# Zero rows only for tokens that no expert keeps, stored under the branch behind the slots, and two small clearings that close the slots' work

## The chip, the cores and the metric

The kernel runs on one core of a Trainium2 chip. The metric is the time of one execution on the device, in microseconds; lower is better. The core has five engines with instruction streams of their own: TensorE (PE in the profile, its weight loads PEld), VectorE (DVE), ScalarE (ACT), GpSimd (POOL) and SyncE (SP). POOL and SP also issue most of the DMAs. The engines wait for each other, and for DMAs, through semaphores. A letter q behind an engine's name (POOLq) is its sequencer, which runs branches, register loads, waits and the issue of DMAs.

## The reference

Attention with a threshold, then a mixture of experts in which each token goes to one expert and an expert keeps at most `capacity` tokens. A token that is not kept gets a row of zeros.

```python
# q, k, v: 4 batches x 8 heads x 576 x 64; tau 0.02; 2304 tokens, DM 512, 8 experts, F 1024, capacity 576
scores = q @ k.T / sqrt(64)
scores = where(scores >= max(scores) - tau, scores, -1e9)
x = (exp(scores - max) / sum) @ v                      # rows of 512 per token
expert = argmax(x @ w_gate); gate_w = softmax(x @ w_gate)[expert]
for i in range(2304):                                  # in order of the tokens
    if counts[expert[i]] < capacity: keep[i] = True; counts[expert[i]] += 1
out = zeros((2304, 512))
out[i] = gate_w[i] * (relu(x[i] @ w1[e]) @ w2[e])      # for kept tokens only, e = expert[i]
```

## The kernel before

**Stages.** Attention runs first, for 16 pairs of heads. The gate then gives each token its expert and its rank in it (`emit_gate1` to `emit_gate2`), and GpSimd scatters the rows of x into a buffer `xd` in device memory, sorted by expert (`emit_scatter`, tiles `xr` and `xrt`). The experts' work is done in 21 slots of 128 rows. Slots 0 to 7 are early ones, one for each expert, whose rows are known before the last batch is done. Slots 8 to 20 are late ones (tiles `latey`, `latex`, `hw`, `lateh`); tables that VectorE works out when the counts of all experts are known (`emit_most` to `emit_own`) say which rows and which expert's weights they take. Ten more slots exist as code behind branches (`slow`), for counts that 21 slots don't cover.

**A slot.** GpSimd gathers its rows from `xd` (`emit_gather`), TensorE turns them (`emit_x0`), ScalarE and VectorE split the result into two float16 parts (`emit_x1`, `emit_x2`). F is cut into four chunks. For each chunk c TensorE multiplies by w1 (`emit_a`), ScalarE and VectorE take the ReLU and split it (`emit_h1`, `emit_h2`), for late slots SyncE turns it by a DMA (`emit_hT`), TensorE multiplies by w2 (`emit_b`), and ScalarE (first chunk) or VectorE (the others) adds the scaled result up in the row buffer (`emit_y`). After the last chunk GpSimd stores the slot's rows to their tokens with an indirect DMA (`emit_out`). `scales` (L420) reads gathered rows of late slots in two goes, of eight slots and of five.

**Weights.** Each of the 8 experts' w1 and w2 chunks is a load of 512 KB (`load_w`, issued at L294, tile `ws`, four buffers) that ScalarE and VectorE split into two float16 parts (`split_w`, L305 and L307, tiles `w1b`, `w2b`). The first 14 loads go over SyncE, the other 50 over GpSimd. In the first chunk a split is cut into two halves. "w2 of expert 6" below is that of the first chunk.

**Order.** No order is written out. `Plan.run` simulates the engines with durations, dependencies and priorities given by `T(...)`, and emits the tasks in the order that comes out. A task that is added, removed or given another duration can therefore change the order of all later tasks on every engine. On an engine the order is fixed then: an instruction that waits holds all behind it.

**Zeros.** A row of the output that no slot stores must be zero. In the kernel before, six DMAs (`clear`, L610, 768 KB each) write zeros to the whole output in the middle of the slots' work, and the first `emit_out` comes after them.

**The end.** After the planned work the code goes on with `slow(13)`: a branch (L1417) on the number of half slots, `nhalves`, that is read from the table `nhi` (`emit_nhi`, `emit_nhalves`) to a register of each engine. If it isn't taken, an engine jumps over the slow code to a block that brings its semaphores up to the counts that the slow code would have left, and then to the barrier that closes the program (L1469).

Of the kernel before, what the change touches and what calls it, by code (L numbers as in the profile page):

```python
# [10 lines left out]
F32 = mybir.dt.float32  # L11
# [4 lines left out]
ALU = mybir.AluOpType  # L16
AX = mybir.AxisListType
# [3 lines left out]
P = 128  # L21
QK_SCALE = 64.0
X_SCALE = 16.0
W_SCALE = 64.0
OOB = float(1 << 22)
MC = 4096.0
ROUND = float(2 ** -20)


def view(ap, dims, offset=0):  # L30
    return bass.AP(tensor=ap.tensor, offset=ap.offset + offset, ap=[ap.ap[0]] + [list(d) for d in dims])
# [138 lines left out]
def attention_moe_kernel(ctx: ExitStack, tc: tile.TileContext, q, k, v, tau, w_gate, w1, w2, cap, out):  # L170
    nc = tc.nc
    B, H, S, D = q.shape
    NTOK, DM = out.shape
    E, _, F = w1.shape
# [32 lines left out]
    def const_of(name, shape, dt=F32):  # L207
        return const.tile([P] + shape, dt, name=name)
# [17 lines left out]
    fst = const_of("fst", [5, E])  # L226
    gie = const_of("gie", [E], I32)
    oix = const_of("oix", [NS], I32)
    gsc = const_of("gsc", [NS])

    make_identity(nc, ident)
# [47 lines left out]
    def disjoint(group, ins):  # L279

        i = getattr(ins, "ins", ins)
        tc.declare_no_dep(i, group=group, reason="disjoint rows")
        tc.add_to_no_dep_group(group, i)
# [152 lines left out]
    def open_tables():  # L436
        def tile_of(name, shape, dt=F32):
            tb[name] = pools["tab"].tile([P] + shape, dt, name=name, tag=name)

        for name, shape in (  # L440
            ("most", [E]), ("cut", [NU2 + 1]), ("bl", [2, NU2 + 1]), ("dv", [2, NU2]), ("alone", [1]), ("u", [SLOTS]),
            ("w", [SLOTS]), ("ge", [NL, NU2]), ("pr", [2, NL, NU2]), ("sel", [2, SLOTS]), ("bad", [SLOTS]), ("ex", [SLOTS]),
            ("own", [3, NP]), ("nhs", [1]),
        ):
            tile_of(name, shape)
        for name, shape in (("left", [E]), ("cnt", [NU2]), ("gix", [SLOTS]), ("exi", [SLOTS]), ("nhi", [1])):
            tile_of(name, shape, I32)
        V.memset(tb["cut"][:, 0:1], 0.0)
        V.memset(tb["bl"][:, 0, NU2:], float(1 << 20))
        V.memset(tb["bl"][:, 1, NU2:], 1.0)  # L450
# [122 lines left out]
    def emit_nhi():  # L573
        U = tb["cut"][:, NU2:]
        V.tensor_scalar(out=tb["nhs"], in0=U, scalar1=tb["alone"], scalar2=None, op0=ALU.add)
        V.scalar_tensor_tensor(out=tb["nhi"], in0=U, scalar=2.0, in1=tb["nhs"], op0=ALU.mult, op1=ALU.min)

    def emit_regs(t):
        r = nc.values_load_multi_w_load_instructions(
# [2 lines left out]
        )[1][0]  # L582
        regs.append(r if t < NE + NF else (r, (t - NE - NF) * WE))

    def emit_nhalves():
        gst["nhalves"] = nc.values_load_multi_w_load_instructions(
            tb["nhi"][0:1, 0:1], min_val=0, max_val=2 * SLOTS + E,
            skip_runtime_bounds_check_because="only a comparison reads it",
        )[1][0]

# [14 lines left out]
        )  # L605
        disjoint("out", ins)

    def clear(z, n):

        nc.gpsimd.dma_start(  # L610
            out=out[z * n:(z + 1) * n, :].rearrange("(p t) d -> p t d", p=P),
            in_=view(zero[:, :], [[0, DM // P * n // P], [1, P]]),
        )


    actx = ExitStack()
    if True:
# [357 lines left out]
        def emit_gate1(b, j):  # L975
            G, n = (NJ, P) if j == 0 else (1, P)
            gp = gps.pop((b, j))
            lg = gp[0:n, 2 * P:2 * P + G * E].rearrange("p (g e) -> p g e", e=E)
            rk_ps = gp[0:n, 2 * P + NJ * E:2 * P + (NJ + G) * E].rearrange("p (g e) -> p g e", e=E)
            sm = xp.tile([P, 6, NJ], F32, name="sm", tag="sm")  # L980
            mx, fe, gs, rk, ix, dp = (sm[0:n, i, 0:G] for i in range(6))
            tb = xp.tile([P, 3, NJ, E], F32, name="tb", tag="tb")
            t0, t1, t2 = (tb[0:n, i, 0:G, :] for i in range(3))
            oh = xp.tile([P, NJ + 1, E], F16, name="oh", tag="oh")
            os = oh[0:n, NJ if G > 1 else 0, :]
            oh = oh[0:n, 0:G, :]
            V = nc.vector
            V.tensor_reduce(out=mx, in_=lg, axis=AX.X, op=ALU.max)
            V.tensor_tensor(out=t0, in0=lg, in1=bc(mx, G, n), op=ALU.subtract)
            gst[b, j] = (G, n, rk_ps, mx, fe, gs, rk, ix, dp, t0, t1, t2, oh, os)  # L990
            gst["os", b, j] = TAIL if j else P, os
            gst["bank"] = gp
# [275 lines left out]
        def at(n):  # L1268
            return NU + PM["B0"] + n * PM["SL"]
# [12 lines left out]
        def V1(name, dur, fn, deps, p=0):  # L1282
            T(name, "V", dur, fn, deps, pt + p)
# [26 lines left out]
            V1(("ex", i), 60 + 17 * m, partial(emit_ex, t), [("ge", i)], p + .5)  # L1310
            V1(("exi", i), 280, partial(emit_exi, t), [("ex", i)], p + .5)
        V1(("own",), 600, emit_own, [("gix", 1), ("bad", 1)], 1)
        V1(("nhi",), 280, emit_nhi, [("alone",)], 2)
        for t in range(NE, NS):
            T(("regs", t), "P", 120, partial(emit_regs, t), [("exi", 0 if t - NE < first.stop else 1), ("gather", t)], at(t - NE))
        T(("nhalves",), "G", 500, emit_nhalves, [("nhi",), ("gather", NE)], pt)

        busy = {b: [("swap_p",)] for b in range(2, 8)}
        busy[0], busy[1] = [("xe", NPR - 1, 2), ("r", NPR - 1, 2)], [("most",), ("lim",)]
        T(("swap_p",), "X", 0, swap_p, [("p", NPR - 1, i) for i in range(6)] + [("max", NPR - 1, i) for i in SI], 0)  # L1320

        def take(bank, *release):
# [18 lines left out]
        for c in range(NCH):  # L1341
            for i in range(2):
# [26 lines left out]
                for t in range(NS):  # L1369
# [30 lines left out]
                    else:  # L1400
# [3 lines left out]
                        e = "A" if c == 0 and PM["yA"] else "V"  # L1404
                        T(("y", c, t), e, 580 if e == "A" else 602, partial(emit_y, c, t, e), [("B", c, t), ("scales", t // GR), ("x0", t)], o('y'), kind="psum")
                        if c == NCH - 1:
                            T(("out", t), "G", 1040, partial(emit_out, t), [("y", c, t)] + ([("clear", z) for z in range(6)] if t == 0 else []), o('out'), dma=730, kind="rows")
        for z in range(6):
            T(("clear", z), "G", 1081, partial(clear, z, NTOK // 6), [("B", 0, PM["clear"])], at(pos - NS + z + PM["clearp"]), dma=2180, kind="rows")
        plan.run()  # L1410
    mctx.close()


    def slow(t):
        if t == SLOTS:
            return
        with tc.If(gst["nhalves"] > 2 * NF + NP + 2 * (t - NL)):  # L1417
            if t == NL:
                m = slice(NL, SLOTS)
                for f in (emit_u, emit_w1, emit_w2, emit_ge, emit_pr, emit_sel, emit_row, emit_gix, emit_bad, emit_ex):  # L1420
                    f(m)
                emit_exi(m, 0)
                regs[NE] = (0, WE)
            emit_gather(NE, tb["gix"][:, t:t + 1])
            emit_x0(NE, 2)
            emit_x1(NE)
            emit_x2(NE)
            scales(gst["late"], NE, 1, tb["bad"][:, t:t + 1])
            ev = [nc.sync.value_load(tb["exi"][p:p + 1, t:t + 1], min_val=0, max_val=E - 1) for p in (0, HP)]
            for c in range(NCH):  # L1430
                for i in range(2):
                    for z in range(2):
                        load_w(i, c, ev[z], nc.sync, z)
                        split_w(i, z)
                emit_a(NE, 3)
                emit_h1(NE)
                emit_h2(NE)
                emit_hT(NE, 1)
                emit_b(NE, 4)
                emit_y(c, NE)  # L1440
            emit_out(NE)
            slow(t + 1)

    slow(NL)


_INS = ["q", "k", "v", "tau", "moe_w_gate", "moe_w1", "moe_w2", "moe_capacity"]
# [25 lines left out]
```

## Time and profile before

| what | us |
|---|---|
| median of 3 runs (lowest, highest) | 658.95 (658.88, 670.36) |
| the profiled execution | 658.05 |
| its span in the profile | 656.3 |
| TensorE busy | 565.5 |
| VectorE busy | 448.3 |
| ScalarE busy | 363.0 |
| GpSimd busy | 329.9 |

The span runs from the first to the last instruction of the profile; 1.75 us of the execution lie outside. The profiled execution is 0.9 us below the median of the three runs. TensorE has the most work, 86% of the span, but with stretches of waiting in it, so that what a change is worth depends on the stretch in which it acts. Times in the profile are counted from the span's start.

### The profile page before, as it was taken

How to read it: one execution, taken by the hardware profiler on the slowest of the kernel's cores; microseconds unless marked ns; L12 is line 12 of the kernel's file. 1: busy time of each engine (PE TensorE's matmuls, PEld its weight loads, DVE VectorE, ACT ScalarE, POOL GpSimd, SP SyncE). 2: the span in 40 equal slices, each digit the busy share in tenths (PEclk: the TensorE clock that was granted, in tenths of full speed). 3: DMA queues.
4: the chain of work that ended last, by engine and by line, in shares of the span. 5: the costliest groups of instructions: out<-in, count | busy, mean ns of one | idle time of the engine just before them, and what ended most of it. 6: DMA issues, size and time to landing. Idle time of an engine off the chain costs nothing. (4 is left out here: it accounts for less than half of the span.)

```text
span 656.3 us, 15955 instructions
## 1 busy us (share of the span) xinstructions
PE 565.5 (86%) x5990; PEld 380.5 (58%) x5990; DVE 448.3 (68%) x957; ACT 363.0 (55%) x551; POOL 329.9 (50%) x323
## 2 busy tenths in 40 slices
PE   0667989999799998999796968799999999889992
PEld 0224656766567665666566827665864586358641
DVE  4657978888677797877968587453558575647452
ACT  5348878888777687574485554466542154216200
POOL 6227877959767388673787247215212021201173
PEclk9979999999989899998997868899999999989997
DMA  6878768755768376671162396959999369924542
GB/s 157 178 162 155 129 113 159 136 123 127 162 127 147 55 164 128 110 110 42 51 208 83 120 292 179 240 119 309 276 183 229 110 141 172 232 75 139 130 186 75
DMA packets 172429, 98.97 MB, mean 151 GB/s; under 512 B 147124, under 2 KB 159480, under 8 KB 172347
## 3 DMA queue, kind: packets, MB, share of 16 engines
q1 hardware_dynamic: 157450, 50.47, 41.7%
q0 software_dynamic: 13600, 46.51, 23.7%
q8 instruction: 52, 0.85, 0.5%
q10 hardware_dynamic: 1296, 0.89, 0.4%
q14 instruction: 31, 0.25, 0.2%
HBM read 53.25 MB, written 14.96 MB: 104 GB/s over the span
## 5 line engine op out<-in xcount | busy, mean ns | idle before, releaser
L760 PE MATMUL s<-kT,qT 128*128 128x512 f16 (+2 forms) x576 | 99.3, 309 | 38.4 <-DMA kT<-kn 25.4
L787 DVE TENSOR_REDUCE mx<-s 128x1 f32<-128x512 f32 x144 | 94.6, 680 | 26.2 <-PE s L760 25.2
L294 POOL DMA_DIRECT2D ws<-in_moe_w_dram x50 | 36.7, 736 | 150.5 <-DVE w2b L307 69.4
L852 DVE SCALAR_TENSOR_TENSOR w2b<-d,ntau,w2b 128x1024 f32<-128x1024 f32 x80 | 101.5, 1277 | 8.0 <-ACT w2b L848 7.8
L822 POOL TENSOR_TENSOR p<-w2b,p 128x1024 f16<-128x1024 f32 x42 | 89.6, 2134 | 20.0 <-ACT p L818 19.5
L760 PE MATMUL d<-qT,kT 128*128 128x512 f16 (+2 forms) x576 | 86.6, 303 | 5.9 <-DVE w2b L852 5.1
L377 PE MATMUL b<-w1b,latex 128*128 (+2 forms) x816 | 81.8, 276 | 5.9 <-DVE latex L352 4.4
L848 ACT ACTIVATE w2b<-d 128x1024 f32<-128x1024 f32 x80 | 80.9, 1020 | 9.0 <-PE d L760 7.9
L760 PEld LDWEIGHTS <-qT 128*128 128x128 f16 (+1 forms) x640 | 39.6, 105 | 66.7 <-issue 29.0
L377 PEld LDWEIGHTS <-latex 128*128 128x128 f16 (+1 forms) x816 | 63.3, 102 | 22.5 <-DVE latex L352 4.8
L760 PEld LDWEIGHTS <-kT 128*128 128x128 f16 (+1 forms) x640 | 37.4, 103 | 47.9 <-issue 28.5
L868 PE MATMUL xo<-v,w2b 128*128 128x65 f32 x256 | 55.6, 300 | 0.0
L413 PEld LDWEIGHTS <-lateh 128*128 128x128 f16 (+1 forms) x408 | 30.9, 103 | 42.5 <-issue 10.2
L307 DVE SCALAR_TENSOR_TENSOR w1b<-ws,w1b 128x1024 f16<-128x1024 f32 (+1 forms) x40 | 45.5, 1146 | 13.4 <-ACT w1b L305 13.4
L307 DVE SCALAR_TENSOR_TENSOR w2b<-ws,w2b 128x1024 f16<-128x1024 f32 (+1 forms) x40 | 39.8, 1006 | 18.7 <-ACT w2b L305 18.5
L370 PEld LDWEIGHTS <-w1b 128*128 128x128 f16 x768 | 47.3, 102 | 8.2 <-issue 6.0
L370 PE MATMUL b<-earlyx,w1b 128*128 128x128 f16 x768 | 51.2, 228 | 0.5 <-DVE w1b L307 0.5
L822 POOL TENSOR_TENSOR w1b<-w2b,w1b 128x1024 f16<-128x1024 f32 x22 | 46.9, 2134 | 8.7 <-ACT w1b L818 8.5
L818 ACT ACTIVATE p<-w2b 128x1024 f16<-128x1024 f32 x42 | 44.3, 1054 | 10.9 <-DVE w2b L852 10.6
L868 PEld LDWEIGHTS <-p 128*128 128x128 f16 x1008 | 43.7, 102 | 10.8 <-issue 1.7
L305 ACT ACTIVATE w1b<-ws 128x1024 f16<-128x1024 f32 (+1 forms) x40 | 34.1, 881 | 27.1 <-DMA ws<-in_moe_w_dram 27.0
L305 ACT ACTIVATE w2b<-ws 128x1024 f16<-128x1024 f32 (+1 forms) x40 | 34.1, 880 | 25.2 <-DMA ws<-in_moe_w_dram 23.5
(207 smaller groups left out, 1058.8 us busy)
## 6 DMA issues: line engine op xcount, KB each, us to landing
ws<-in_moe_w_dram POOLq DMA_DIRECT2D x50, 512.0 KB, 7.3
ws<-in_moe_w_dram SPq DMA_DIRECT2D x14, 512.0 KB, 5.6
out_dram<-zero POOLq DMA_DIRECT2D x6, 768.0 KB, 11.9
kr<-in_k_dram SPq DMA_DIRECT2D x15, 256.0 KB, 2.9
qr<-in_q_dram SPq DMA_DIRECT2D x14, 256.0 KB, 3.0
v<-in_v_dram SPq DMA_DIRECT2D x28, 128.0 KB, 3.0
qr<-in_q_dram ACTq DMA_DIRECT2D x2, 256.0 KB, 4.0
v<-in_v_dram POOLq DMA_DIRECT2D x4, 128.0 KB, 3.5
```

What stands on the lines that cost most here:

```text
L294: eng.dma_start(out=t, in_=src)
L305: nc.scalar.activation(out=dst[:, :, 0, :], in_=t, func=AF.Copy, scale=W_SCALE)
L307: nc.vector.scalar_tensor_tensor(out=dst[:, :, 1, :], in0=t, scalar=W_SCALE, in1=dst[:, :, 0, :], op0=ALU.mult, op1=ALU.subtract)
L370: nc.tensor.matmul(out=hp[:, f * P:(f + 1) * P], lhsT=wb[0][:, o:o + P], rhs=xT[t][:, xi], start=(d == 0 and z == 0), stop=(d == NB - 1 an ...
L377: nc.tensor.matmul(out=hp[m, 0:FC], lhsT=xT[t][:, xi, m], rhs=wb[0][:, bass.ds(r + (2 * d + wi) * FC, FC)], start=(d == 0 and z == 0), sto ...
L760: nc.tensor.matmul(out=out, lhsT=l, rhs=r, start=(z == 0), stop=(z == 1), **kw)
L787: V.tensor_reduce(out=m[:, i, 0:1], in_=ps_s[i % 2], axis=AX.X, op=ALU.max)
L818: nc.scalar.activation(out=p16_of(s, k)[:, 0], in_=p32_of(s, k), func=AF.Copy)
L822: eng.tensor_tensor(out=p[:, 1], in0=p32_of(s, k), in1=p[:, 0], op=ALU.subtract)
L848: nc.scalar.activation(out=t, in_=d, func=AF.Exp, scale=sc_s)
L852: V.scalar_tensor_tensor(out=t, in0=d, scalar=ntau, in1=t, op0=ALU.is_ge, op1=ALU.mult)
L868: nc.tensor.matmul(out=ps_x[:, j * DV:j * DV + r.shape[-1]], lhsT=l, rhs=r, start=(z == 0), stop=(z == len(ops) - 1))
```

## The change

- `clear` and its six tasks go, and with them the wait of the first `emit_out`.
- The ranks of all tokens, a temporary before, are kept in a table `rks`.
- `emit_over` is new on VectorE: two instructions on 8 numbers find whether an expert has more tokens than it keeps, as 0 or 4096 in `most1`. `emit_nhi` gets two instructions more and leaves two numbers: `nhi[1]` is the old number of half slots, `nhi[0]` the larger of that and `most1`.
- The branch behind the slots is now taken if `nhi[0]` is over 22. In it, `zero_rows` works out the tokens that aren't kept and stores zeros to them by 20 indirect DMAs, the others' indices being out of bounds; then `nhi[1]` is read and the old branches of `slow` follow.
- Behind the planned work, ahead of the branch, stand two clearings: VectorE sets `alone` to 0 (128 x 1), GpSimd one number of `exi`.

```diff
+FAR = 4096.0
...
+    rks = const_of("rks", [B, NJ + 1])
...
     def emit_nhi():
         U = tb["cut"][:, NU2:]
         V.tensor_scalar(out=tb["nhs"], in0=U, scalar1=tb["alone"], scalar2=None, op0=ALU.add)
-        V.scalar_tensor_tensor(out=tb["nhi"], in0=U, scalar=2.0, in1=tb["nhs"], op0=ALU.mult, op1=ALU.min)
+        V.scalar_tensor_tensor(out=tb["nhs"], in0=U, scalar=2.0, in1=tb["nhs"], op0=ALU.mult, op1=ALU.min)
+        V.tensor_copy(out=tb["nhi"][:, 1:2], in_=tb["nhs"])
+        V.tensor_tensor(out=tb["nhi"][:, 0:1], in0=tb["nhs"], in1=tb["most1"], op=ALU.max)
...
+    def emit_over():
+        V.tensor_scalar(
+            out=tb["over"], in0=ps_g[:, 512 - E:], scalar1=cap_f, scalar2=FAR, op0=ALU.is_gt, op1=ALU.mult
+        )
+        V.tensor_reduce(out=tb["most1"], in_=tb["over"], axis=AX.X, op=ALU.max)
+
...
-    def clear(z, n):
-
-        nc.gpsimd.dma_start(
-            out=out[z * n:(z + 1) * n, :].rearrange("(p t) d -> p t d", p=P),
-            in_=view(zero[:, :], [[0, DM // P * n // P], [1, P]]),
-        )
-
+    def zero_rows():
+
+        t, z, lost = tb["zix"], tb["tokens"], tb["lost"]
+        nc.gpsimd.iota(t[:, :, 0:NJ], pattern=[[S, B], [1, NJ]], base=0, channel_multiplier=NJ)
+        nc.gpsimd.iota(t[:, :, NJ:], pattern=[[S, B], [0, 1]], base=NJ * P, channel_multiplier=1)
...
+        V.tensor_scalar(out=lost, in0=rks, scalar1=cap_f, scalar2=OOB, op0=ALU.is_lt, op1=ALU.mult)
+        V.tensor_tensor(out=t, in0=lost, in1=z, op=ALU.add)
+        V.memset(y[0][:, 0:DM], 0.0)
+        for b in range(B):
+            for j in range(NJ + 1):
+                ins = nc.gpsimd.indirect_dma_start(
+                    out=out[:, :], out_offset=bass.IndirectOffsetOnAxis(ap=t[:, b, j:j + 1], axis=0),
+                    in_=y[0][:, 0:DM], in_offset=None, bounds_check=NTOK - 1, oob_is_err=False,
+                )
+                disjoint("out", ins)
...
-            sm = xp.tile([P, 6, NJ], F32, name="sm", tag="sm")
-            mx, fe, gs, rk, ix, dp = (sm[0:n, i, 0:G] for i in range(6))
+            sm = xp.tile([P, 5, NJ], F32, name="sm", tag="sm")
+            mx, fe, gs, ix, dp = (sm[0:n, i, 0:G] for i in range(5))
+            rk = rks[0:n, b, j:j + G]
...
-        V1(("nhi",), 280, emit_nhi, [("alone",)], 2)
+        V1(("over",), 300, emit_over, [("tot",), ("swap",)], 0.2)
+        V1(("nhi",), 420, emit_nhi, [("alone",), ("over",)], 2)
...
-        busy[0], busy[1] = [("xe", NPR - 1, 2), ("r", NPR - 1, 2)], [("most",), ("lim",)]
+        busy[0], busy[1] = [("xe", NPR - 1, 2), ("r", NPR - 1, 2)], [("most",), ("lim",), ("over",)]
...
-                            T(("out", t), "G", 1040, partial(emit_out, t), [("y", c, t)] + ([("clear", z) for z in range(6)] if t == 0 else []), o('out'), dma=730, kind="rows")
-        for z in range(6):
-            T(("clear", z), "G", 1081, partial(clear, z, NTOK // 6), [("B", 0, PM["clear"])], at(pos - NS + z + PM["clearp"]), dma=2180, kind="rows")
+                            T(("out", t), "G", 1040, partial(emit_out, t), [("y", c, t)], o('out'), dma=730, kind="rows")
         plan.run()
+        V.memset(tb["alone"], 0.0)
+        nc.gpsimd.memset(tb["exi"][0:1, 0:1], 0)
     mctx.close()
...
-        with tc.If(gst["nhalves"] > 2 * NF + NP + 2 * (t - NL)):
+        with tc.If(gst["nhs"] > 2 * NF + NP + 2 * (t - NL)):
...
-    slow(NL)
+    with tc.If(gst["nhalves"] > 2 * NF + NP):
+        zero_rows()
+        gst["nhs"] = nc.values_load_multi_w_load_instructions(
+            tb["nhi"][0:1, 1:2], min_val=0, max_val=2 * SLOTS + E,
+            skip_runtime_bounds_check_because="only comparisons read it",
+        )[1][0]
+        slow(NL)
```

**What moves on GpSimd at the late gathers.** The row `latey<-xd,gix` is a gather of a late slot, `ws<-in_moe_w_dram` with 128x2x512 a load of w2, here that of expert 6 and then that of expert 7; `nhi` is the load of the branch's register. Before:

```order
L1059 DMA xd<-xrt,ixi 36864x257
L294 DMA ws<-in_moe_w_dram 128x2x512
L335 DMA latey<-xd,gix 128x514 x5
L586 TENSOR_LOAD nhi
L335 DMA latey<-xd,gix 128x514 x8
L294 DMA ws<-in_moe_w_dram 128x2x512
L294 DMA ws<-in_moe_w_dram 128x4x256 x8
```

After:

```order
L1082 DMA xd<-xrt,ixi 36864x257
L337 DMA latey<-xd,gix 128x514 x4
L596 TENSOR_LOAD nhi
L337 DMA latey<-xd,gix 128x514 x8
L296 DMA ws<-in_moe_w_dram 128x2x512
L337 DMA latey<-xd,gix 128x514
L296 DMA ws<-in_moe_w_dram 128x2x512
L296 DMA ws<-in_moe_w_dram 128x4x256 x8
```

The load for expert 6 stood ahead of all 13 gathers; now it stands behind the twelfth, and the last gather behind it.

**What moves on ScalarE in the late slots' first products.** `latex` is `emit_x1` of a late slot, `hw` is `emit_h1` of one, and `w2b<-ws` x2 is the split of one expert's w2. Before, with the split of expert 7 in it (that of expert 6 stands some way ahead):

```order
L347 ACTIVATE latex<-b_4838 128x512
L392 ACTIVATE hw<-b_4840 128x256
L347 ACTIVATE latex<-b_4837 128x512
L392 ACTIVATE hw<-b_4841 128x256
L347 ACTIVATE latex<-b_4838 128x512
L305 ACTIVATE w2b<-ws 128x512 x2
L392 ACTIVATE hw<-b_4839 128x256
L347 ACTIVATE latex<-b_4837 128x512
```

After:

```order
L394 ACTIVATE hw<-b_4847 128x256
L349 ACTIVATE latex<-b_4843 128x512
L394 ACTIVATE hw<-b_4845 128x256
L349 ACTIVATE latex<-b_4844 128x512
L307 ACTIVATE w2b<-ws 128x512 x2
L394 ACTIVATE hw<-b_4846 128x256
L349 ACTIVATE latex<-b_4843 128x512
L307 ACTIVATE w2b<-ws 128x512 x2
L394 ACTIVATE hw<-b_4847 128x256
```

In slots: before, the split of expert 7 stood behind `latex` of slot 13, ahead of `hw` of slot 12. Now the split of expert 6 stands ahead of `hw` of slot 10 and `latex` of slot 12, and that of expert 7 ahead of `hw` of slot 11 and `latex` of slot 13. TensorE's order changes with it in one place that the prediction uses: the product with w2 of the early slot 4 (`emit_b`, six matmuls) moves from behind all of the late slots' first products to a place ahead of them.

**What moves on GpSimd at the end.** `out_dram<-latey,oix` is `emit_out` of a late slot; the last rows are the block behind the branch, the branch out of it, and the barrier. Before, from the last block of catching up:

```order
L1417 ISA
L1417 UNCONDITIONAL_BRANCH
L602 DMA out_dram<-latey,oix 2304x512
L1469 UNCONDITIONAL_BRANCH
L1469 ISA
```

After:

```order
L1468 ISA
L1468 UNCONDITIONAL_BRANCH
L1434 MEMSET exi 1x1
L1499 UNCONDITIONAL_BRANCH
L1499 ISA
```

Before, the store of slot 20 stood behind the branch and its catching up (12 of the 13 late stores stood ahead of the branch); now all 13 stand ahead of it, and the one instruction behind it is the clearing of `exi`. On VectorE, `emit_y` of slot 20 stood behind the branch too, and now stands ahead of it, with the clearing of `alone` after it.

## Rows read from the trace of the kernel before

**Rows 1.** Stretches: us, sum, busy of PE, PEld, DVE, ACT, POOL (x instructions), PEclk, DMA, GB/s.

```profile
385.00:400.00 15.00, 10.27 (x46) 5.48 (x46) 14.45 (x63) 8.18 (x15) 7.86 (x7) 0.61 0.77 236
...
435.00:465.00 30.00, 30.00 (x253) 17.01 (x252) 12.35 (x14) 20.21 (x31) 11.90 (x14) 1.00 0.91 274
465.00:490.00 25.00, 24.02 (x275) 19.59 (x273) 14.69 (x24) 13.45 (x26) 5.89 (x8) 1.00 1.01 212
```

**Rows 2.** Chain that ended last: start us, us, what.

```profile
434.88 1.40 PE b L413 x6
...
472.95 10.57 DMA ws<-in_moe_w_dram
```

**Rows 3.** Timeline of the end: start us, us, engine, line [idle before <-releaser].

```profile
643.29 1.46 PE L413 MATMUL gp<-w2b,lateh 128*64 x12
643.50 0.75 DVE L599 SCALAR_TENSOR_TENSOR latey<-b,gsc,latey 128x512 f32<-128x512 f32 x1 [0.54 <-PE b L413]
...
644.52 0.97 POOL L602 DMA_INDIRECT out_dram<-latey,oix  x1 [0.33 <-DVE latey L599]
646.54 0.75 DVE L599 SCALAR_TENSOR_TENSOR latey<-gp,gsc,latey 128x512 f32<-128x512 f32 x1 [2.29 <-PEq L1417]
650.03 0.97 POOL L602 DMA_INDIRECT out_dram<-latey,oix  x1 [4.54 <-DMA out_dram<-latey,oix]
```

**Rows 4.** The branch's line L1417: queue, operation, duration ns min/median/max, starts.

```profile
L1417 POOLq EVENT_SEMAPHORE  x4: 17/43/43, 647.6 to 647.8; - x4
...
L1417 PEldq COMPARE_BRANCH  x1: 4005/4005/4005, 642.3 to 642.3; - x1
...
L1417 POOLq INC_SWDGE_SEM  x1: 1260/1260/1260, 647.9 to 647.9; - x1
```

**Rows 5.** The closing barrier's line L1469, the same columns.

```profile
L1469 POOLq DRAIN  x3: 51/115/5680, 649.8 to 656.0; - x3
```

**Rows 6.** The clearing's line L610 and its landings.

```profile
L610 POOL DMA_DIRECT2D out_dram<-zero x6: 1009/1130/1360, 447.8 to 455.2; - x6
...
DMA to landing us min/median/max: 7.2/11.9/14.9
```

**Rows 7.** TensorE's timeline where it next waits after the clearing.

```profile
486.25 3.26 PE L377 MATMUL b<-w1b,latex 128*64 x48 [0.98 <-DVE hw L396]
```

**Rows 8.** DMA queues from 619.5 us to the end: packets, MB, share.

```profile
q0 software_dynamic: 1680, 4.72, 33.7%
```

**Rows 9.** VectorE's timeline around the slot tables.

```profile
394.59 1.29 DVE L307 SCALAR_TENSOR_TENSOR w2b<-ws,w2b 128x512 f16<-128x512 f32 x2
...
415.24 0.17 DVE L420 SCALAR_TENSOR_TENSOR oix<-bad,latey 128x5 int32<-128x5 f32 x1 [4.24 <-DMA latey<-xd,gix]
```

**Rows 10.** GpSimd's timeline: load, last gather, next loads.

```profile
389.35 0.78 POOL L294 DMA_DIRECT2D ws<-in_moe_w_dram  x1 [1.84 <-DVE bl L490]
...
409.60 1.00 POOL L335 DMA_INDIRECT latey<-xd,gix  x1 [0.30 <-DVE latex L352]
410.60 3.07 POOL L294 DMA_DIRECT2D ws<-in_moe_w_dram  x4
```

**Rows 11.** Landing of the load issued at 389.35.

```profile
DMA to landing us min/median/max: 5.0/5.0/5.0
```

**Rows 12.** ScalarE's timeline: the split it waits with, and what follows.

```profile
418.09 1.15 ACT L305 ACTIVATE w2b<-ws 128x512 f16<-128x512 f32 x2 [4.66 <-DMA ws<-in_moe_w_dram]
419.14 0.36 ACT L392 ACTIVATE hw<-b 128x256 f16<-128x256 f32 x1
419.41 0.59 ACT L347 ACTIVATE latex<-b 128x512 f16<-128x512 f32 x1
```

**Rows 13.** TensorE's timeline over the late slots' first products.

```profile
416.22 2.03 PE L377 MATMUL b<-w1b,latex 128*128 x11 [3.31 <-DVE latex L352]
...
418.90 2.24 PE L377 MATMUL b<-w1b,latex 128*128 x12
```

**Rows 14.** Landings of all 45 weight loads issued by GpSimd after 420.

```profile
DMA to landing us min/median/max: 3.9/7.2/14.4
```

More of the change, by code (lines that the diff above doesn't have):

```diff
@@ L442, in open_tables @@
             ("w", [SLOTS]), ("ge", [NL, NU2]), ("pr", [2, NL, NU2]), ("sel", [2, SLOTS]), ("bad", [SLOTS]), ("ex", [SLOTS]),
-            ("own", [3, NP]), ("nhs", [1]),
+            ("own", [3, NP]), ("nhs", [1]), ("over", [E]), ("most1", [1]), ("lost", [B, NJ + 1]), ("tokens", [B, NJ + 1]),
         ):
             tile_of(name, shape)
-        for name, shape in (("left", [E]), ("cnt", [NU2]), ("gix", [SLOTS]), ("exi", [SLOTS]), ("nhi", [1])):
+        for name, shape in (("left", [E]), ("cnt", [NU2]), ("gix", [SLOTS]), ("exi", [SLOTS]), ("nhi", [2]), ("zix", [B, NJ + 1])):
             tile_of(name, shape, I32)
@@ L583, in emit_regs @@
         regs.append(r if t < NE + NF else (r, (t - NE - NF) * WE))
+    def emit_over():
[3 more added lines that the diff above has]
+        V.tensor_reduce(out=tb["most1"], in_=tb["over"], axis=AX.X, op=ALU.max)
     def emit_nhalves():
         gst["nhalves"] = nc.values_load_multi_w_load_instructions(
-            tb["nhi"][0:1, 0:1], min_val=0, max_val=2 * SLOTS + E,
+            tb["nhi"][0:1, 0:1], min_val=0, max_val=int(FAR),
             skip_runtime_bounds_check_because="only a comparison reads it",
@@ L606, in emit_out @@
         disjoint("out", ins)
-    def clear(z, n):
-        nc.gpsimd.dma_start(
-            out=out[z * n:(z + 1) * n, :].rearrange("(p t) d -> p t d", p=P),
-            in_=view(zero[:, :], [[0, DM // P * n // P], [1, P]]),
-        )
+    def zero_rows():
+        t, z, lost = tb["zix"], tb["tokens"], tb["lost"]
+        nc.gpsimd.iota(t[:, :, 0:NJ], pattern=[[S, B], [1, NJ]], base=0, channel_multiplier=NJ)
+        nc.gpsimd.iota(t[:, :, NJ:], pattern=[[S, B], [0, 1]], base=NJ * P, channel_multiplier=1)
+        V.tensor_copy(out=z, in_=t)
+        V.scalar_tensor_tensor(
+            out=z[:, :, NJ], in0=half[:, 0:1].to_broadcast([P, B]), scalar=OOB, in1=z[:, :, NJ], op0=ALU.mult, op1=ALU.add
+        )
+        V.tensor_scalar(out=lost, in0=rks, scalar1=cap_f, scalar2=OOB, op0=ALU.is_lt, op1=ALU.mult)
[8 more added lines that the diff above has]
+                disjoint("out", ins)
     actx = ExitStack()
```

## The prediction

> **What bounds the kernel now.** I read the stretches first, then the chain of waits, then the timelines where the change acts. From 435 to 465 TensorE is busy all 30 of 30 us, at full clock, and from 465 to 490 for 24.02 of 25 [rows 1]: this is the part in which the six clearings are issued, at 447.8 to 455.2, and land 7.2 to 14.9 us later [rows 6]. So TensorE's own work sets the pace there. From 385 to 400 it is busy only 10.27 of 15 us, at a mean granted clock of 0.61 [rows 1]: here the slot tables, the gathers and the first weights set the time, and the change moves instructions in just this stretch. At the end, TensorE starts its last product at 643.29, which is over at 644.75, and the program runs to 656.3 [rows 3]: the last 11.5 us are a chain on GpSimd's queue. In order: the store of slot 19 starts at 644.52; the block behind the branch waits for it until 647.6 (a landing of 3.05 us) and then spends 1.26 us on a semaphore instruction; only then does the store of slot 20 start, at 650.03, and the barrier's drain on GpSimd, begun at 649.8, takes 5.68 us, to 655.5 [rows 3 to 5]. The last 0.84 us are the barrier.
>
> **The end: a gain of 4.2 us.** Before, the `emit_y` of slot 20 waits on TensorE's sequencer, whose branch takes 4.0 us from 642.3, and so starts at 646.54 [rows 3, 4]. The change puts it and its store ahead of the branch. The product is over at 644.75; `emit_y` starts 0.05 later, at 644.80, and from the start of one `emit_y` to the start of its store are 1.02 us (643.50 to 644.52) [rows 3], so the store starts at 645.82 instead of 650.03, 4.21 earlier. What is late next? The block behind the branch still waits for the last store: 645.82 + 3.05 = 648.87, plus 0.32 and 1.26 as before, 650.45; then the clearing of `exi`, for which I take 0.2 (small operations are under that), 650.7, and the drain. Whether the drain is long does not follow from the trace: the long one stood around a store. Counted from the start of the last store it ended 5.46 us later, which gives 645.82 + 5.46 = 651.28, just behind the 650.7 of the other chain. I take this: **-4.2 us**. Bounds: with a drain as short as the other two of its line (0.05 and 0.115 [rows 5]) the gain is 4.7; if it is counted from the end of the semaphore instruction (649.15 to 655.5, 6.35), it ends at 656.8 and the end is 1.3 us later than before. I choose the first because the drain began before the store did and outlasted it.
>
> **The clearings: -0.5 us.** Six times about 1.13 us on GpSimd and 4.7 MB of stores go [rows 6]. GpSimd's time is covered: TensorE doesn't wait once between 435 and 465 [rows 1]. The first wait after it is 0.98 us at 486.25 [rows 7], behind a weight load that took 10.57 us from its issue at 472.95 [rows 2]; the last clearing landed at about 470, when other loads were queued, so the backlog ahead of that load may get shorter. The gain lies between 0 and 0.98; I take the middle. Later waits start from products after this one and don't move with it.
>
> **The new instructions on VectorE: nothing.** Four small ones, in a chain of such with 0.1 to 0.25 us each, stand in the tables' part. In exchange the second half of the split of expert 2's w2 now stands behind the tables, so the tables end about where they did, at 394.6 [rows 9], and that half split of 0.6 us follows. TensorE waits for it, and starts the next product about 1 to 2 us later than before. I charge nothing for this, since TensorE runs into the next, longer wait anyway; its cover is that wait.
>
> **The moved load: +2.3 us.** This is the term that costs. Before, the load of w2 of expert 6 is issued at 389.35 and lands 5.0 us later [rows 10, 11], long before its split. Now it takes the place that the last gather had, 409.60 [rows 10], then 0.78 for it, 0.3 for the gap, 1.0 for the last gather, so that expert 7's load is issued at 411.7 instead of 410.60. ScalarE meets these splits in its queue, with `hw` of slot 10 and `latex` of slot 12 behind the first and those of 11 and 13 behind the second. How long such a load takes at that place is shown by expert 7's: issued at 410.60, it was waited for by ScalarE until 418.09 [rows 10, 12], 7.5 us. With 7.5 the two land at 417.1 and 419.2. From the first landing: two halves of the split 1.15, `hw` 0.38, `latex` 0.60 [rows 12], and VectorE's part of `latex` with 0.68, some 2.85 us until TensorE can go on with slot 12: 419.95. From there to slot 13's product are 2.68 us (416.22 to 418.90 [rows 13]): 422.6. The second landing allows slot 13 at 419.2 + 2.85 = 422.05, so the first decides. Before, slot 13 began at 418.90: 3.7 us later. But `emit_b` of slot 4, some 1.4 us [rows 2], is done by then and lay behind the late slots before: 3.7 - 1.4 = **+2.3**. The wait of 4.24 us that VectorE has before for the last five gathers [rows 9], which holds TensorE for 3.31 at 416.22 [rows 13], is not added: the last gather lands while the two loads do, and VectorE asks for it only after slot 12. Bounds: with the 5.0 of the earlier load slot 13 starts at 420.1, and the term is -0.2; with the 10.57 of the slow load [rows 2] at 425.7, and it is +5.4. I take 7.5, as it is from the same place in the queue and the same neighbours.
>
> [...]
>
> **The branch is not taken.** From 619.5 on the DMAs of GpSimd's queue move 4.72 MB [rows 8]; 2304 rows of 2048 bytes are 4.719 MB. So every token is stored, none is over its expert's capacity, and `zero_rows` doesn't run.
>
> **The sum.** Against the profiled execution, 658.05: -4.2 - 0.5 + 2.3 = -2.4, 655.65. The median of the runs is 0.9 higher, and the new time is a median too: 658.95 - 2.4 = **656.5 us**. A measurement of this kernel can tell about 2% from no change, here 13 us; every term above is well under that.
>
> **Rivals.**
> 1. The end isn't shortened, because GpSimd's drain counts from the semaphore instruction. Place: the barrier; price: +1.3 in place of -4.2. Then 658.95 + 1.3 - 0.5 + 2.3 = 662.0, slower than before. It decides as soon as the end gains less than the 1.8 us that the other terms cost. For it: the drain began 0.7 after that instruction's end; against it: a store lay between. Chance 0.12.
> 2. The moved loads are as slow as the slow one, 10.57: 658.95 - 4.2 - 0.5 + 5.4 = 659.7, no gain. For it: SyncE's turning DMAs and two other loads run at the same time. Chance 0.14.
> 3. The moved loads are quick, 3.9: slot 13 would begin at 409.6 + 3.9 + 2.85 + 2.68 = 419.0, the term is 0.1 - 1.4 = -1.3, and the time 658.95 - 4.2 - 0.5 - 1.3 = 653.0. For it: with expert 6's load away from 389, the early loads and the scatter have less beside them. [...] Chance 0.14.
> 4. The change doesn't do what it says and the branch is taken: 20 stores of 0.97 + 0.33 us [rows 3] on GpSimd, 26 us, and landing and code behind them, some 30: about 687. The 4.72 MB speak against it. Chance 0.02.
>
> My forecast has the other 0.58. The range goes over the first three rivals except its outermost part: from 652.5 to 661.5. Faster by over 2% would be below 645.8, which no case gives: 0.02, for what I haven't seen. Slower by over 2% is above 672: rival 4 and as much unseen, 0.03. Within 2%: 0.95.
>
> **What would show it.** In the profile of the changed kernel: 13 late stores about 1.3 us apart with the last at 645 to 648 and no gap before it; the drain of GpSimd over within 6 us of it; no row of `zero`; ScalarE waiting on `ws` twice in the late slots' first products, and TensorE for 5 us or so ahead of slot 12; TensorE without waits through the place of the clearings. The prediction is wrong if ScalarE doesn't wait there, if the drain's end stays at its distance from the semaphore instruction, or if a wait appears that I don't have: the branch's register is loaded earlier on TensorE and ScalarE, and is held there until VectorE has `nhi`.

## The result, and the profile after

| | before | after |
|---|---|---|
| median of the runs, us | 659.43 (658.88 to 670.36, four runs) | 637.92 (632.86 to 642.98, four runs) |
| the profiled execution, us | 658.05 | 642.98 |
| its span, us | 656.3 | 641.3 |

The ratio is 0.9625, with a 95% interval of 0.957 to 0.968: the changed kernel is 3.2 to 4.3% faster, where 0.4% was forecast. The profiled execution of the changed kernel is the slowest of its four runs and a disturbed one (mean granted clock 0.938 against 0.943 to 0.947 in the other three), as are those of e1, e3, e4 and e5 below, so that the ratios leave them out; the rows of after come from its trace, in which the gain is 15 us.

The stage that the prediction watched is no better than it was. In the trace of the changed kernel it lies 13 us earlier. This is one stretch of it, with the columns of [rows 1]:

```profile
372.00:386.00 14.00, 8.09 (x21) 2.67 (x21) 13.59 (x65) 6.40 (x11) 6.50 (x6) 0.62 0.69 210
```

TensorE is busy 8.09 of 14 us, at a mean granted clock of 0.62, against 10.27 of 15 and 0.61 before [rows 1]. The 13 us were gained ahead of it, in attention, where the two kernels run the same instructions in the same order. What differs there is a duration. These are SyncE's turning DMAs of attention before (kT, then qT; ns min/median/max, first and last start):

```profile
L742 SPq DMA_TRANSPOSE kT<-kn x16: 2510/2763/3667, 14.2 to 285.0; - x16
L747 SPq DMA_TRANSPOSE qT<-qn x16: 2702/2808/3679, 11.3 to 290.8; - x16
```

and after:

```profile
L764 SPq DMA_TRANSPOSE kT<-kn x16: 1911/2339/3258, 13.3 to 270.2; - x16
L769 SPq DMA_TRANSPOSE qT<-qn x16: 1910/2190/3699, 11.2 to 275.7; - x16
```

A turn holds SyncE's queue 0.4 to 0.6 us less in the median. The 48 turns of attention (these 32 and 16 shorter ones) add up to 116.4 us of SyncE before and to 97.2 after. TensorE waits for them: of the line of the products of q and k, the idle time of its matmuls by what ended it (us, times), in the first 330 us before:

```profile
  DMA kT<-kn: 25.4, 4
  DMA qT<-qn: 7.8, 4
```

and in the 317 us that the same work takes after:

```profile
  DMA kT<-kn: 21.3, 3
  DMA qT<-qn: 0.8, 2
```

So 33.2 us of waiting became 22.1. Most of what is left is the start of the program, where the first matmul waits for the first loads and turns, before and after:

```profile
18.77 2.81 PE L760 MATMUL s<-kT,qT 128*128 128x512 f16 x6 [18.77 <-DMA kT<-kn]
17.49 2.81 PE L782 MATMUL s<-kT,qT 128*128 128x512 f16 x6 [17.49 <-DMA kT<-kn]
```

Behind this first wait, 14.4 us became 4.7. The last row maximum of attention (`mx`) starts at 328.7 before and at 315.8 after, 12.9 us earlier (the last number of each line, before and after):

```profile
L793 DVE TENSOR_REDUCE mx<-gp x16: 214/216/225, 27.6 to 328.7; 128x1 f32<-128x64 f32 x16
L815 DVE TENSOR_REDUCE mx<-gp x16: 214/216/225, 26.1 to 315.8; 128x1 f32<-128x64 f32 x16
```

The table `nhi` is written 12.9 us earlier too: all of it is there when the late slots begin.

At the end of the program, the timeline after, with the rows that answer to [rows 3]:

```profile
631.64 1.46 PE L415 MATMUL gp<-w2b,lateh 128*64 x12
...
633.15 0.75 DVE L609 SCALAR_TENSOR_TENSOR latey<-gp,gsc,latey 128x512 f32<-128x512 f32 x1 [0.54 <-PE gp L415]
633.44 0.97 POOL L612 DMA_INDIRECT out_dram<-latey,oix  x1 [0.30 <-issue]
633.85 0.06 DVE L1433 MEMSET alone<- 128x1 f32 x1
634.72 0.97 POOL L612 DMA_INDIRECT out_dram<-latey,oix  x1 [0.30 <-POOLq L1468]
639.17 0.09 POOL L1434 MEMSET exi<- 1x1 int32 x1 [3.48 <-DMA out_dram<-latey,oix]
```

and the semaphore instruction of the branch's line, which answers to [rows 4]:

```profile
L1468 POOLq INC_SWDGE_SEM  x1: 460/460/460, 638.6 to 638.6; - x1
```

and the closing barrier's, which answers to [rows 5]:

```profile
L1499 POOLq DRAIN  x3: 46/109/1252, 639.2 to 641.0; - x3
```

The stores go out 1.28 us apart and the last of them no longer waits for the branch (the 0.30 us that its row puts down to L1468 stand ahead of the other stores too). From the end of TensorE's last product to the end of the span are 8.12 us (633.11 to 641.23) against 11.55 (in both without the last 0.03 us, a semaphore instruction of TensorE's weight loads). But the drain is 1.25 us instead of 5.68, and the semaphore instruction 0.46 instead of 1.26, neither of which the prediction had.

### The profile page after: what moved, and what is told of

It is laid out like the page before. It is cut to its first block, busy times and chain, and to the rows that moved or that the text cites. A ratio compares the mean times of both kernels' runs of the same rounds, so it can differ in the third digit from the quotient of the medians.

```text
span 641.3 us, 15966 instructions
## 1 busy us (share of the span) xinstructions
PE 568.5 (89%) x5990; PEld 381.1 (59%) x5990; DVE 448.4 (70%) x962; ACT 362.2 (56%) x551; POOL 323.9 (51%) x318
## 4 chain that ended last, share of the span: by engine, by line
PE 49%; DMA 15%; DVE 14%; issue 12%; POOL 4%; ACT 4%; SPq 2%; POOLq 0%; ACTq 0%; DVEq 0%
PE xo L890 10%; PE s L782 9%; PE d L782 7%; DMA ws<-in_moe_w_dram 7%; PE b L372 5%; DVE w2b L874 4%; PE b L379 3%; PE xo L415 3%; PE b L415 3%; PE gp L415 3%; PE gp L956 3%; PE xo L902 2%; DVE mx L809 2%; DMA out_dram<-latey,oix 2%; POOL out_dram L612 2%
## 5 line engine op out<-in xcount | busy, mean ns | idle before, releaser
L782 PEld LDWEIGHTS <-kT 128*128 128x128 f16 (+1 forms) x640 | 37.2, 103 | 46.2 <-issue 26.7
L372 PEld LDWEIGHTS <-w1b 128*128 128x128 f16 x768 | 45.5, 100 | 7.9 <-issue 5.5
L372 PE MATMUL b<-earlyx,w1b 128*128 128x128 f16 x768 | 49.1, 224 | 0.5 <-DVE w1b L309 0.5
```

Source lines behind the costliest of these rows:

```text
L372: nc.tensor.matmul(out=hp[:, f * P:(f + 1) * P], lhsT=wb[0][:, o:o + P], rhs=xT[t][:, xi], start=(d == 0 and z == 0), stop=(d == NB - 1 an ...
L782: nc.tensor.matmul(out=out, lhsT=l, rhs=r, start=(z == 0), stop=(z == 1), **kw)
```

## The experiments

**Where the change acts by accident.** `rks` is a new table ahead of the two weight buffers in the allocation, 80 bytes per partition and 96 with the rounding. Every tile that is allocated behind it on that side lies 96 bytes further on. In the program's allocation the first `kn`, a source of the turns, starts at byte 111008 of a partition before, which is 216 times 512 and 416 over, and at 111104 after, which is 217 times 512. **Theory A** is that this makes the gain. **Theory B** is that the edits make it which the prediction weighed: the clearings, the load, the end.

The experiments ran on three chips, on which single runs of the kernel before lay between 661 and 692 us, so that of the times only ratios to it on the same chip are compared; small terms are read from the traces. The table has, for each trace, where `kn` starts behind a multiple of 512 bytes, the median turn of kT, the last row maximum, and three distances: from `nhi` written to the first product of a late slot with w2, from there to the end of the last product, and from there to the end of the span (us).

| kernel | kn at | kT turn | last `mx` | nhi to lateh | to last product | to end |
|---|---|---|---|---|---|---|
| before | 416 | 2.76 | 328.7 | 46.5 | 204.7 | 11.55 |
| after | 0 | 2.34 | 315.8 | 47.4 | 205.0 | 8.12 |
| e1_pad96 | 0 | 2.27 | 316.5 | 48.6 | 208.6 | 15.25 |
| e2_after_shift | 416 | 2.76 | 333.5 | 51.5 | 201.7 | 9.16 |
| e3_tail | 416 | 2.74 | 330.4 | 48.7 | 216.9 | 14.03 |
| e4_noclear | 416 | 2.76 | 335.7 | 50.9 | 203.7 | 11.11 |
| e5_pad32 | 448 | 2.78 | 330.0 | 46.6 | 208.0 | 11.38 |
| e6_pad352 | 256 | 2.34 | 316.0 | 46.6 | 206.1 | 11.41 |
| e7_turn_only | 0 | 2.37 | 315.6 | 46.2 | 204.9 | 11.42 |
| e8_turn_back | 416 | 2.73 | 328.9 | 47.0 | 205.1 | 11.80 |
| e9_load_back | 0 | 2.39 | 315.8 | 50.5 | 209.6 | 8.85 |
| e10_after_again | 0 | 2.39 | 316.2 | 47.3 | 204.3 | 9.28 |
| e11_late_aligned | 0 | 2.19 | 316.5 | 49.2 | 203.2 | 9.16 |
| e12_sync_clear | 416 | 2.71 | 333.8 | 48.6 | 221.9 | 11.01 |

How far one trace can be trusted is seen from kernels that are alike in a stage. Those with the clearings on GpSimd take 204.7 to 216.9 us in the middle, those without any 201.7 to 209.6. The turns and the last row maximum fall into two groups without overlap: 2.19 to 2.39 us and 315.6 to 316.5 us with `kn` at 0 or 256, 2.71 to 2.78 and 328.7 to 335.7 at 416 or 448. Why the end of e1 takes 15.25 us isn't shown.

**e1_pad96.**

```diff
     oix = const_of("oix", [NS], I32)
+    pad = const_of("pad", [B, NJ + 1])
```

> The kernel before with one table more, 96 bytes per partition, that nobody reads or writes, at the place where the change puts rks. No instruction is added, removed or moved; only the tiles allocated behind it lie 96 bytes further on, among them kn and qn, the sources of the turning DMAs of attention, which then start at a multiple of 512 bytes (before: 416 past one). Theory A (the addresses make the gain): the gain of attention is here too, 13 to 15 us, so about 645 us, and SyncE's kT turns take about 2.3 us in the median instead of 2.76. Theory B (the removed clearings, the moved load and the end make it): no change, 659 us.

Measured: ratio to the kernel before 0.9726 (0.9574 to 0.9877). The turns are those of the changed kernel:

```profile
L743 SPq DMA_TRANSPOSE kT<-kn x16: 1907/2268/3241, 13.3 to 272.6; - x16
```

and the last row maximum starts 12.2 us earlier than before. Ninety-six bytes that nobody touches are worth 1.2 to 4.3%; Theory B has no place for this.

**e2_after_shift.**

```diff
     rks = const_of("rks", [B, NJ + 1])
+    pad = const_of("pad", [104])
```

> The changed kernel with 416 bytes of padding behind rks, so that all tiles behind it lie 512 bytes further on than in the kernel before, at the same place within 512 bytes; its instructions are those of the changed kernel. Theory A: the gain of attention goes, and what is left is what the instructions do: the prediction's sum, 656.5 us, within 653 to 658. Theory B: it stays at about 638 us.

Measured: ratio 0.9896 (0.9816 to 0.9976). Most of the gain is gone, and the turns are back at the old duration:

```profile
L765 SPq DMA_TRANSPOSE kT<-kn x16: 2500/2764/3767, 14.2 to 287.8; - x16
```

What is left, 0.2 to 1.8%, can be what the instructions of the change do: the prediction's sum, 656.5 of 658.95, is 0.996 and lies in this interval. It isn't shown, since e8 below, with the instructions of the kernel before, comes out as much faster.

**e3_tail.**

```diff
         plan.run()
+        V.memset(tb["alone"], 0.0)
+        nc.gpsimd.memset(tb["exi"][0:1, 0:1], 0)
```

> The kernel before with nothing but the two closing clearings behind the planned work, by which the last emit_y and the last store come ahead of the branch. Prediction's term: -4.2 us, 654.8 us; from the changed kernel's trace, where 8.2 us instead of 11.6 lie between the end of the last product and the end of the span: -3.4, 655.6. The rival that GpSimd's drain counts from its semaphore instruction: +1.3, 660.3.

Measured: no ratio was formed; its six runs lie at 663 to 680 us and those of the kernel before at 662 to 692, so that the time settles nothing. The trace does. The last store went out ahead of the catching up, yet its semaphore instruction took 1.28 us, and the drain of the closing line, with no store in it, is still long:

```profile
L1419 POOLq INC_SWDGE_SEM  x1: 1280/1280/1280, 666.5 to 666.5; - x1
...
L1471 POOLq DRAIN  x3: 51/115/4600, 667.8 to 673.0; - x3
```

**e4_noclear.** It leaves out the zeros for tokens that no expert keeps; there are none here.

```diff
-                            T(("out", t), "G", 1040, partial(emit_out, t), [("y", c, t)] + ([("clear", z) for z in range(6)] if t == 0 else []), o('out'), dma=730, kind="rows")
-        for z in range(6):
-            T(("clear", z), "G", 1081, partial(clear, z, NTOK // 6), [("B", 0, PM["clear"])], at(pos - NS + z + PM["clearp"]), dma=2180, kind="rows")
+                            T(("out", t), "G", 1040, partial(emit_out, t), [("y", c, t)], o('out'), dma=730, kind="rows")
```

> The kernel before without the six clearings; it leaves out the zeros for tokens that no expert keeps (there are none here), and the order of all other instructions is the old one. Prediction's term: -0.5 us (0 to -0.98), 658.5 us. Theory B would have to find a good part of the 21 us here: 650 us or less.

Measured: ratio 0.994 (0.9878 to 1.0002): no gain of the size that Theory B needs, and from nothing to 1.2% otherwise. In the middle, from the first product of a late slot with w2 to the last product, it takes 203.7 us against 204.7 with the clearings, a difference well inside the scatter. At the end its semaphore instruction takes 0.44 us instead of 1.26, and the drain, with a store in it as before, 3.51 instead of 5.68:

```profile
L1415 POOLq INC_SWDGE_SEM  x1: 440/440/440, 661.2 to 661.2; - x1
...
L1467 POOLq DRAIN  x3: 51/109/3510, 662.3 to 666.4; - x3
```

**e5_pad32 and e6_pad352** move the same tiles by other amounts, 32 and 352 bytes.

```diff
     oix = const_of("oix", [NS], I32)
+    pad = const_of("pad", [8])     # e5; [88] in e6
```

> The kernel before with 32 bytes of unused padding where the change puts rks: kn and qn start at 448 past a multiple of 512 bytes, a multiple of 64 but not of 128. If a multiple of 64 bytes is enough, this is as quick as the 96 bytes (3% under the kernel before, kT turns of 2.3 us in the median, the last row maximum of attention some 13 us earlier). If the 256-byte pieces that a turn reads must not cross a multiple of 256, nothing is gained: turns of 2.76 us, the time of the kernel before.

> The kernel before with 352 bytes of unused padding at the same place: kn and qn start at 256 past a multiple of 512 bytes. If a multiple of 256 is enough, the whole gain of the 96 bytes is here (turns of 2.3 us, 3% under the kernel before); if it takes 512, nothing or part of it.

Measured: e6 has a ratio of 0.9742 (0.9655 to 0.9829). For e5 none was formed; its four runs go from 651 to 684 us, those of the kernel before from 661 to 670, so that only its trace (of a run of 662.75) speaks, and why one run was as quick as 651 is open. At 448 a turn of kT takes what it took at 416:

```profile
L743 SPq DMA_TRANSPOSE kT<-kn x16: 2431/2782/3738, 14.2 to 286.1; - x16
```

at 256 what it takes at 0:

```profile
L743 SPq DMA_TRANSPOSE kT<-kn x16: 1868/2338/3341, 13.3 to 270.4; - x16
```

A multiple of 64 bytes is not enough, and 512 is not needed: of the four offsets that were run, the two that are multiples of 256 are fast. An odd multiple of 128 was not tried. kT's turns take 2.19 to 2.39 us in the median at 0, 2.34 at 256, 2.71 to 2.76 at 416 and 2.78 at 448, about a fifth more at the last two. That it comes from pieces which cross a multiple of 256, as the expectation of e5 has it, no trace shows.

**e7_turn_only and e8_turn_back** separate the sources of the turns from everything else that the 96 bytes move. e7 pads ahead of `kn` alone; e8 has the padding of e1 and 416 bytes more ahead of `kn`.

```diff
+        deadp.tile([P, 24], F32, name="pad")      # e7; [P, 104] in e8, beside e1's pad
         kns = [deadp.tile([P, 2, KB, P], F16, name=f"kn{i}") for i in range(NKN)]
```

> The kernel before with 96 bytes of padding directly ahead of kn, so that kn, qn, kT1 and qT1 start at a multiple of 512 bytes, and everything else that the change moves (weights, loads of q and k, early slots) stays where it was. If the turning DMAs make the gain, all of it is here: turns of 2.3 us and 3% under the kernel before. If the other moved tiles make it: the time of the kernel before.

> The opposite: 96 bytes of padding where the change puts rks, and 416 more ahead of kn, so that the weights, their loads, those of q and k and the early slots start at a multiple of 512 bytes, and kn, qn, kT1 and qT1 at 416 past one, as before. If the turning DMAs make the gain: turns of 2.76 us and the time of the kernel before. If the other tiles make it: 3% under it.

Measured: for e7 no ratio was formed, but all of its four runs, 640 to 657 us, lie below the quickest of the kernel before, 661; e8 has a ratio of 0.9887 (0.9796 to 0.9977). In the traces e7 has the whole gain of attention:

```profile
L743 SPq DMA_TRANSPOSE kT<-kn x16: 1920/2366/3191, 13.4 to 273.3; - x16
```

with its last `mx` at 315.6, and e8 has none of it, with the last `mx` at 328.9:

```profile
L744 SPq DMA_TRANSPOSE kT<-kn x16: 2491/2728/3646, 14.1 to 285.2; - x16
```

So it is the turns. e7 moves `kT1` and `qT1`, one of three destinations, along with the sources; but in the trace after, the turns into the two destinations that did not move got shorter as much (mean turn of kT into each of its three buffers: 2.58, 2.34, 2.27 us, of which only the second lies at a new place; before 3.02, 2.85, 2.83). The sources decide. That e8 is 0.2 to 2% faster with turns as before has no counterpart in its trace, which ends at 657.1; this stays open.

**e9_load_back and e10_after_again** ask for the price of the moved load.

```diff
-        V1(("over",), 300, emit_over, [("tot",), ("swap",)], 0.2)
+        V1(("over",), 0, emit_over, [("tot",), ("swap",)], 0.2)      # e9
```

> The changed kernel with one number altered: the planned time of the new task over is 0 instead of 300, by which the load of w2 of expert 6 stands again ahead of all 13 late gathers, as in the kernel before; addresses and instructions are those of the changed kernel. Prediction's term: the moved load costs 2.3 us (-0.2 to 5.4), so this should be 2.3 us quicker than the changed kernel, with the time from the slot tables to the first product with w2 of a late slot shorter by as much. The rival that the moved load costs nothing: the same time as the changed kernel within 1 us.

> The changed kernel itself, to stand beside the others on this chip: 3 to 4% under the kernel before.

Measured: e9 has a ratio of 0.9697 (0.962 to 0.9775), e10 of 0.9705 (0.962 to 0.979). It is the planned 0.3 us of a task that moves the load of expert 6 behind twelve gathers, and the move costs nothing that these runs can tell; with intervals of about 5 us to either side they don't exclude the 2.3 us of the prediction. In the traces e9 is the slower one, 50.5 us from the tables to the first product with w2 of a late slot against 47.3; TensorE has gaps from 389 to 397 there, and from 390 to 400 it is busy for 5.86 us at a granted clock of 0.59. I don't count this for the moved load, since the traces with the old order lie at 46.2 to 50.9.

**e11_late_aligned** puts the sources of the late slots' turns at a multiple of 256 too, the one version that the findings point to.

```diff
         r = p.tile([P, n, ROW], F32, name=name + "y")
+        if name == "late":
+            p.tile([P, 24], F32, name="pad")
```

> The changed kernel with 96 bytes of unused padding in the pool of the late slots, so that hw, the source of the 28 turning DMAs of the late slots, and latex, lateh and latey start at a multiple of 256 bytes too (before and after: 96 past one). Those turns hold SyncE 1.26 us in the median in every run so far, and the 9-piece turns of qT, 1.29 us, did not get shorter when their source was moved to a multiple of 256. So nothing should come: the time of the changed kernel within 1%. The rival, that the late slots wait for landings of these turns and gain as attention did, would give 3 us or more.

Measured: ratio 0.963 (0.9542 to 0.9718) beside 0.9705 of e10; the intervals overlap, and it isn't shown to be faster. The late turns don't get shorter:

```profile
L406 SPq DMA_TRANSPOSE lateh<-hw x28: 1189/1258/7870, 405.4 to 603.9; - x28
```

against 1.259 us in the changed kernel. A turn of 8 or 9 pieces takes 1.2 to 1.3 us at every place of its source that was run; those of 18 pieces take 2.71 to 2.78 us for kT at 416 and 448, and 2.19 to 2.39 at 0 and 256.

**e12_sync_clear** issues the clearings from SyncE.

```diff
     def clear(z, n):
-        nc.gpsimd.dma_start(
+        nc.sync.dma_start(
```

> The kernel before with the six clearings issued by SyncE instead of GpSimd, at the same place of the order; the zeros still go to memory, but GpSimd issues six DMAs fewer. It asks why the catching-up instruction at the end takes 1.26 us and the closing drain 4.6 to 5.7 with the clearings, and 0.44 to 0.46 and 1.25 to 3.5 without them. If the number of DMAs that GpSimd issued decides it: 0.44 and 3.5, as in the kernel without the clearings. If the zeros in memory decide it: 1.26 and 5.7, as before. On SyncE the turns of the late slots queue behind the clearings, which can cost some us in the middle.

Measured: ratio 1.0185 (1.0038 to 1.0333, from two runs), so 0.4 to 3.3% slower. Its middle stage takes 221.9 us instead of 204.7, but that this comes from SyncE isn't shown: its longest waits of TensorE, 6.54 us at 519.19 and 7.65 at 577.80, have their like in e3, 8.29 and 6.69, where the clearings are on GpSimd and the middle takes 216.9; and no turn of a late slot stands between the clearings and 17 us after them. The end is that of the kernel without clearings, to the hundredth:

```profile
L1417 POOLq INC_SWDGE_SEM  x1: 440/440/440, 675.4 to 675.4; - x1
```

and

```profile
L1469 POOLq DRAIN  x3: 51/109/3509, 676.5 to 680.6; - x3
```

Zeros are still written here. So what makes these two instructions longer, 1.26 and 5.68 us before against 0.44 and 3.51, isn't the zeros in memory, but that GpSimd issues six DMAs more in its stream.

## Why the prediction was wrong

**The step that failed is the sum.** It runs over the terms of the instructions that were added, removed or moved, from the slot tables on, and takes all 385 us ahead of them as they were, because the same instructions stand there in the same order. The table `rks` came into it only as a place where ranks are kept. That a table moves every tile behind it, and with them the sources of 32 long DMAs for which TensorE waits, was not costed: it is worth 12.9 us in the trace (e1, e6 and e7 have it alone, e2 and e8 are without it). The rivals shared the blind spot: all four act on the instructions, and a gain of over 2% had a chance of 0.02. Its signs of being wrong shared it too: none of them looks at attention.

**Term by term, in the two profiled executions** (656.3 to 641.3, so -15.0):

- Attention: forecast 0, measured -12.9.
- The new VectorE instructions: forecast 0. From the last row maximum to `nhi` written are 64.8 us before and 64.9 after. Right.
- The moved load: forecast +2.3 (-0.2 to 5.4). Its mechanism came as described. After, the load for expert 6 is issued at 395.69 and that for expert 7 behind the last gather (compare [rows 10]):

```profile
395.69 0.80 POOL L296 DMA_DIRECT2D ws<-in_moe_w_dram  x1
396.79 1.05 POOL L337 DMA_INDIRECT latey<-xd,gix  x1 [0.30 <-issue]
397.84 2.34 POOL L296 DMA_DIRECT2D ws<-in_moe_w_dram  x3
```

ScalarE waits for both, with the first products of slots 10 to 13 behind it (compare [rows 12]):

```profile
401.52 1.15 ACT L307 ACTIVATE w2b<-ws 128x512 f16<-128x512 f32 x2 [3.54 <-DMA ws<-in_moe_w_dram]
...
406.62 1.15 ACT L307 ACTIVATE w2b<-ws 128x512 f16<-128x512 f32 x2 [3.18 <-DMA ws<-in_moe_w_dram]
```

and TensorE waits ahead of slots 12 and 13 (compare [rows 13]):

```profile
404.78 2.72 PE L379 MATMUL b<-w1b,latex 128*128 x12 [3.83 <-issue]
...
409.06 1.88 PE L379 MATMUL b<-w1b,latex 128*128 x12 [0.97 <-ACT hw L394]
```

  Counted from `nhi`, slot 13's product starts 3.0 us later than before (28.4 instead of 25.4; forecast 3.7), and `emit_b` of slot 4 is done by then. At the first product with w2 of a late slot +0.9 is left, less than the 4.7 us by which traces with the old order differ there (46.2 to 50.9), so that the size of the term stays open. The first load took 5.8 us to its split and the second 8.8, where 7.5 was taken for both. The 3.9 that the third rival takes is the shortest landing of [rows 14], whose loads were all issued after 420, behind the last gather (409.60), and not beside gathers.
- The clearings in the middle: forecast -0.5. The wait of 0.98 us of [rows 7] is gone, and 4.50 us of waiting stand at 497.46 instead, where before there were 0.97, 0.42 and 1.02:

```profile
497.46 2.72 PE L415 MATMUL xo<-w2b,lateh 128*128 x6 [4.50 <-DVE latey L609]
```

  From the first product with w2 of a late slot to the last product of all are 204.7 us before and 205.0 after: nothing that the scatter of this stage lets one see.
- The end: forecast -4.2, measured -3.4 (8.12 instead of 11.55), and -2.3 in e10 (9.28). The size is near by luck, since the reason was not right. The prediction let the drain hang on the last store, 5.46 us after its start; it did end 5.69 us after it, but as a drain of 1.25 us that begins only when this store has landed and the semaphore instruction is over. By the traces it hangs on two things: with the clearings on GpSimd and a store in it 5.68 (before), with these clearings alone 4.60 (e3), with a store alone 3.51 (e4, e12), with neither 1.25 (after). Removing the clearings takes 2.2 to 3.4 us from the drain and 0.8 from the semaphore instruction, more than moving the store does (1.1 to 2.3). Part of this was lost ahead of it: the last store started 0.55 us later than its row allowed, held by the queue of stores, and landed 3.83 us after its start instead of 3.05.
- The branch is not taken, as forecast: in the last stretch GpSimd's queue again moves 4.72 MB, in 1680 packets [rows 8].

**Where the rivals stand.** That the drain counts from the semaphore instruction (6.34 us from its end to the drain's end before) fell: after, it is 1.31. Loads as slow as 10.57 or as quick as 3.9 did not come, nor did the branch.

**What stays open.** The three runs behind the first ratio lie at 632.86 to 638.21, 5 to 10 us below the execution that was profiled; no trace shows where. The second profiled run of the changed kernel, on another chip, spans 640.1. Of the gain of about 21 us in the medians, 15 are accounted for. By e8 the other tiles that the table moves (weights, their loads, early slots) may be worth part of the rest, 0.2 to 2%, but its trace shows no place for it.

## What to carry to other kernels

A change that allocates a table moves the tiles behind it: compare the addresses of the two programs, not only their instructions, and look first at the tiles that DMAs read in small pieces (here 18 of 256 bytes) and for which an engine waits. A line of the profile in which the busiest engine waits for a DMA (here 33.2 us of matmuls for the turns of q and k, 14.4 of them behind the program's start) is a first price for everything that can alter that DMA's duration, even where no instruction on it was edited. And a kernel whose sources happen to lie right can lose as much by an equally small edit, as e2 did (turns of kT of 2.76 us instead of 2.34, the last `mx` at 333.5 instead of 315.8); put the sources of long turns at a multiple of 256 bytes on purpose, where they took 2.19 to 2.39 us here.

## What the runs showed of the hardware that had not been expected

- A turning DMA of 18 pieces of 256 bytes (from 11.26 to 16.9 us of the trace before, with two such turns alone on the DMA queues, 3585 packets moved 0.91 MB, about 254 bytes each) took SyncE 2.71 to 2.78 us in the median (kT; qT 2.79 to 2.83) with its source at 416 or 448 behind a multiple of 512 bytes, and 2.19 to 2.39 (qT 2.06 to 2.37) at 0 or 256. Turns of 8 or 9 pieces took 1.24 to 1.30 us in every kernel.
- GpSimd's closing drain and its semaphore instruction took longer with the six clearings in GpSimd's stream, which the kernel before issued 190 us and more ahead of them (447.8 to 455.2, against 647.9 and 649.8): the drain 4.6 to 5.7 us and the semaphore instruction 1.26 to 1.28, against 1.25 to 3.5 and 0.44 to 0.46 without them. Which property of those DMAs does it wasn't tried.
